# Pooled attention into a gated MLP on one core: Strassen units in the first product, upper groups first in the second, batch 2 as pooled rows

## Chip, core and metric

The kernel runs on one core of a Trainium2 chip. The metric is device time in microseconds (us): 296.05 us, the median of three runs (296.0 to 296.78). TensorE is called PE below, VectorE DVE, ScalarE ACT, GpSimd POOL and SyncE SP. PE and its weight loads (PEld) are separate rows of the profile.

## What is computed

```python
B, H, S, D = 8, 8, 576, 64            # attention; pool = 8, so 72 pooled keys
k_p = k.reshape(B, H, 72, 8, D).mean(axis=3)
v_p = v.reshape(B, H, 72, 8, D).mean(axis=3)
attn = softmax(q @ k_p.T / sqrt(D))   # 576 x 72 for each head
x = (attn @ v_p) -> (4608, 512)       # heads side by side
h = x @ w_in                          # 512 -> 2048
out = (h * sigmoid(h)) @ w_out        # 2048 -> 512, float32
```

Matrix operands are bf16 on the chip, sums are float32.

## The kernel before

**Tiles.** The 4608 tokens are worked through in nine tiles of 512 (NTT), t = 0 to 8. Each tile has two stages. `up` computes the hidden layer of the tile, h_T, in 16 groups of 128 hidden units: four matmuls of 128x512 a group (the four parts of d_model), then one Silu on ACT, which reads PSUM and writes h_T in bf16. `down` (tile 0) or `down_quarters` (tiles 1 to 8) computes the output rows.

**Second product.** `down_quarters` is Strassen's scheme (its form with fewer additions is kept in three PSUM tiles P, Q and R). The hidden layer is cut in four quarters (two halves of the tokens, two halves of the hidden units: groups 0 to 7 and 8 to 15), w_out likewise. Seven products replace eight. Each is 16 matmuls of 128x256; product n takes its left operand from h_sum[n] (a sum of two quarters of h_T, made on DVE by `hidden_sum(n, k0, k1)` for the groups k0 to k1 of a half) or from h_T, and its right operand from w_out or from w_sum (made once, by `weight_sum`). The order is 2, 5, 1, 4, 3, 7, 6. P, Q and R are used again as soon as DVE has read them: r_sb is a copy of product 2, rr_sb = Q + r_sb, t_sb = R - rr_sb, and o_sb gets P, Q, P + t_sb and Q + t_sb.

**Attention.** While PE works on tile t, it also does the attention of batch a = t + 1 (576 tokens each, so batches and tiles drift apart). Per batch: K and V are pooled on DVE, K is brought to kz (transposed by PE through kT_ps, copied by DVE), q is transposed by DVE in four parts (`q_transpose`), and four visits (two halves of the tokens f, two groups of four heads g) each do `scores` (PE, then four exponentials on ACT into es), `denominators` (PE into den_ps, then Ln and Exp on ACT into rec) and `numerators` (PE into nu_ps, then DVE into xT, which is the first product's input).

**Pooling.** Batches 0 and 1 are loaded as pooled rows (`load_slots`): row (head, pooled key) on the 128 partitions, five slots of them, its eight source rows side by side, 2 KB. `slot_sums` adds the eight on DVE in three steps, and small matmuls with an identity or a shift matrix (`select_k`, `select_v`) bring each head's 72 rows to where they are used. Batch 2 is loaded by `load_heads`, with 72 partitions and four heads in a tile (k_raw, k_raw2, v_raw, v_raw2), all eight source rows side by side, once w_out is there; `tree` (lines 197 and 208) adds them on DVE. Later batches are loaded by `load_one` (first four source rows) and `load_rest`, a DMA issued by POOL that adds the other four in flight, so that DVE has one step less.

**Order.** The order within an engine is written by hand. `up` and the downs count their matmuls in steps (64 and 112), and a list of fillers (f_up, f_down) says behind which step other work is put: (36, f) runs f behind step 36; what is left at the end runs then. Each engine works in the order in which the program emits its instructions, so a filler that waits holds up what is behind it on its engine. In `up` before, the groups go 0 to 15, the h_sums are put at steps 20 to 59, and four of them at the end.

**Buffers.** PSUM has eight one-bank tiles: three of tag mm (hp_ps, and P, Q, R of down) and five of tag at (attention). r_sb, rr_sb and t_sb exist once.

Of the kernel before, what the change touches and what calls it, by code (L numbers as in the profile page):

```python
# [27 lines left out]
FP32 = mybir.dt.float32  # L28
# [8 lines left out]
def kernel(  # L37
# [74 lines left out]


# [68 lines left out]

    def load_heads(b, name, tags, behind=None):
        st = batches.setdefault(b, {})
        st[f"{name}_raws"] = []
        for i, tag in enumerate(tags):
            raw = raw_tile(tag, H // 2)
            if behind is not None:
                nc.gpsimd.tensor_copy(out=raw[:, 0, :1], in_=behind)
            load_rows(nc.sync, raw, source(b, name)[:, i * H // 2 : (i + 1) * H // 2, :])  # L190
            st[f"{name}_raws"].append(raw)


    def tree(dsts, raw):
        w = raw.shape[2] // 2
        while w > D:
            nc.vector.tensor_add(  # L197
                out=raw[:, :, :w], in0=raw[:, :, :w], in1=raw[:, :, w : 2 * w]
            )
            w //= 2  # L200
        n = H // 2 if len(dsts) > 1 else raw.shape[1]
        for i, dst in enumerate(dsts):
            in0, in1 = (
                raw[:, i * n : (i + 1) * n, c * D : (c + 1) * D].rearrange(
                    "k h (c d) -> k h c d", c=2
                ) for c in range(2)
            )
            nc.vector.tensor_add(out=dst, in0=in0, in1=in1)


    def pooled(b, name, i):
        p = batches[b][f"{name}p"]
        if name == "k":
            return p[:, i].rearrange("k c s d -> k s c d")
        return p[:, i * H // 2 : (i + 1) * H // 2, :].rearrange(
            "k h (c d) -> k h c d", c=2
        )

    def pool_heads(b, name, i):
        tree([pooled(b, name, i)], batches[b][f"{name}_raws"][i])  # L220

    def pool_k(b, parts=(0, 1)):
        st = batches[b]
        st["kp"] = mid.tile([SP, 2, 2, 4, DH], BF16, tag="kp", bufs=1, name="kp")
        if "k_raws" not in st:
            tree([pooled(b, "k", i) for i in range(2)], st["k_raw"])
        else:
            for i in parts:
                pool_heads(b, "k", i)

    def pool_v(b, parts=(0, 1)):
        st = batches[b]
        st["vp"] = mid.tile([SP, H, D], BF16, tag="vp", name="vp")
        if "v_raws" not in st:
            tree(
                [st["vp"].rearrange("k h (c d) -> k h c d", c=2)], st["v_raw"]
            )
        else:
            for i in parts:
                pool_heads(b, "v", i)  # L240

    def k_transpose(b, parts=(0, 1)):
        st = batches[b]
        kT_ps = ps_tile([128, 2, 2, SP], BF16, "at", "kT_ps")
        for a in parts:
            for c in range(2):
                nc.tensor.transpose(
                    kT_ps[:, a, c, :],
                    st["kp"][:, a, c].rearrange("k s d -> k (s d)"),
                    ident[:SP, :SP],  # L250
                )
        a0, a1 = parts[0], parts[-1] + 1
        nc.vector.tensor_copy(out=kz[b % 2][:, a0:a1], in_=kT_ps[:, a0:a1])
# [14 lines left out]
            raw_tile(f"{n}_raw{i}", H, full=True)[:, : m * RE].rearrange(  # L268
                "r (i e) -> r i e", e=RE
            ) for i, m in (("", SA), (2, SLOTS + 1 - SA))  # L270
# [3 lines left out]
    def load_slots(eng, b, name, i0, i1):  # L274
        src = (k if name == "k" else v)[b].rearrange("h (sp p) d -> (h sp) (p d)", p=POOL)
        tiles = row_tiles[name]
        if i0 == SLOTS:
            eng.dma_start(out=tiles[1][:REST, SLOTS - SA], in_=src[128 * SLOTS :])
        else:
            j = i0 // SA  # L280
            eng.dma_start(
                out=tiles[j][:, i0 - SA * j : i1 - SA * j],
                in_=src[128 * i0 : 128 * i1].rearrange("(i r) e -> r i e", r=128),
            )

    def slot_sums(name, j):
        raw = row_tiles[name][j]
        dst = rows5[name][:, SA:] if j else rows5[name][:, :SA]
        w = RE // 2
        while w > D:  # L290
            nc.vector.tensor_add(  # L291
                out=raw[..., :w], in0=raw[..., :w], in1=raw[..., w : 2 * w]
            )
            w //= 2
        nc.vector.tensor_add(out=dst, in0=raw[..., :D], in1=raw[..., D : 2 * D])
# [120 lines left out]

    def up(t, fillers, items):
        step = spread(fillers, len(items) * KF)
        for g, n0, n in items:
            hp_ps = ps_tile([128, 512], FP32, "mm", "hp_ps")  # L420
            c0 = (t * NTT + n0) % NX

            for r0, r1 in ((0, min(n, NX - c0)), (min(n, NX - c0), n)):
                for kk in range(KF) if r1 > r0 else ():
                    if r0 == 0:
                        next(step)
                    x0 = (c0 + r0) % NX
                    nc.tensor.matmul(  # L428
                        hp_ps[:, r0:r1],
                        lhsT=w_in_sb[:, kk, g * 128 : (g + 1) * 128],  # L430
                        rhs=xT[:, kk, x0 : x0 + r1 - r0],
                        start=(kk == 0), stop=(kk == KF - 1),
                    )
            nc.scalar.activation(h_T[:, g, n0 : n0 + n], hp_ps[:, :n], func=AF.Silu)  # L434
        for _ in step:
            pass

# [84 lines left out]
    def down_quarters(t, fillers, last=False):  # L522
# [7 lines left out]
        def product(n, k0, k1, cs=(0, 1)):  # L530
            b = bank[n]
            for kt in range(k0, k1):
                for c in cs:
# [4 lines left out]
                        stop=kt == KQ - 1, skip_group_check=True,  # L538
# [5 lines left out]
        KA = KQ - 2  # L544
        product(2, 0, KA)
        product(5, 0, KA)
        product(2, KA, KQ)
        nc.vector.tensor_copy(out=r_sb, in_=ps["P"])
        product(5, KA, KQ)
        tt(out=rr_sb, in0=ps["Q"], in1=r_sb, op=add)  # L550
        for cc in ((0,), (1,)) if last else ((0, 1),):
# [4 lines left out]
            nc.vector.tensor_copy(out=o_sb[1][:, cs, LO], in_=ps["P"][:, cs])  # L556
# [105 lines left out]

    visits = [(f, g) for f in range(2) for g in range(2)]
    for t in range(NT):
# [11 lines left out]
        else:  # L676
            items = [(g, 0, NTT) for g in range(KG)]
            for n, k0, k1, at in (
                (6, 0, 4, 20), (6, 4, 8, 36),
                (2, 0, 4, 51), (5, 0, 4, 52), (1, 0, 4, 53), (2, 4, 6, 58), (5, 4, 6, 59),  # L680
            ):
                f_up.append((at, lambda n=n, k0=k0, k1=k1: hidden_sum(n, k0, k1)))
            f_up.append((64, lambda: hidden_sum(2, 6, 8)))
            f_up.append((64, lambda: hidden_sum(5, 6, 8)))
            f_up.append((64, lambda: hidden_sum(1, 4, 8)))
            f_down.append((27 if t < NT - 1 else 41, lambda: hidden_sum(7, 0, 8)))

        for n, t0, f_to, at in (
            (1, 0, f_down, 48), (3, 0, f_down, 54), (4, 1, f_up, 12),
            (7, 1, f_down, 10), (6, 1, f_down, 50),  # L690
        ):
            for i in range(PW):
                if t == t0:
                    f_to.append((at + i, lambda n=n, i=i: weight_sum(n, i)))
        if a < B:
            q_at = [20, 28, 36, 44] if t else [82, 84, 86, 88]
            if t == 0:
                for j in range(2):
# [5 lines left out]
                    f_down.append((37 + 3 * j, lambda j=j: copy_v(1, j)))  # L704
            else:
                f_up.append((0, lambda: pool_k(a)))
                f_up.append((25, lambda: k_transpose(a)))
            for n in range(4):
                f_up.append((q_at[n], lambda n=n: q_transpose(a, n // 2, n % 2)))
            if t == 1:  # L710
                f_up.append((46, lambda: pool_v(a, (0,))))
                f_down.append((30, lambda: pool_heads(a, "v", 1)))
            elif t:
                f_up.append((10, lambda: pool_v(a)))
            if t == 0:
                f_down.append((0, lambda: load_q(2)))

                last = w_out_sb[:SP, KG - 1, d_model - 1 :]
                f_down.append(
                    (1, lambda: load_heads(2, "k", ("k_raw", "k_raw2"), last))  # L720
                )
                f_down.append(
                    (14, lambda: load_heads(2, "v", ("v_raw", "v_raw2"), last))
                )
            elif a + 1 < B:
                f_v = f_up if t > 1 else f_down
# [3 lines left out]
                f_v.append((11 if t > 1 else 31, lambda: load_one(a + 1, "v")))  # L730
                f_v.append((12 if t > 1 else 32, lambda: load_rest(a + 1, "v")))
# [11 lines left out]
            for n, (f, g) in enumerate(visits):  # L743
                if n < 3 or not 3 <= t < B - 2:
                    f_down.append((nu_at[n], lambda f=f, g=g: numerators(a, g, f)))
# [36 lines left out]
```

The softmax here doesn't subtract the row's maximum and nothing guards it: scores larger than these inputs give would overflow.

## Time and profile before

| | us |
|---|---|
| device time, median of 3 | 296.05 |
| profiled span | 294.7 |
| PE busy | 287.9 |
| DVE busy | 191.2 |
| ACT busy | 177.6 |
| POOL busy | 42.8 |

The busy row of a page says how long an engine had something in work. Matmuls are pipelined, and their ends are modelled: a busy PE may still wait. Where it is full can be read from the distance between the starts of consecutive matmuls. The chain of waits follows the work back from the last instruction; a long run of one engine in it, with no other between, means that this engine alone set the time there. The table of stretches gives the busy time of each engine in each tile.

### The profile page before, as it was taken

The numbers are of one execution on the slowest core, as the hardware profiler recorded it, in microseconds if no ns is written. First come the engines' busy times: TensorE is split into PE (matmuls) and PEld (weight loads), VectorE is DVE, ScalarE is ACT, GpSimd is POOL, SyncE is SP. The second block draws the span as 40 slices with busy tenths as digits, with TensorE's granted clock in tenths as the row PEclk, the third lists the DMA queues.
The fourth block names the chain that finished last, engine by engine and source line by source line (L and its number), as shares of the span: only waits on it lengthen the run. The fifth ranks groups of instructions, "written<-read, shape, count | busy, mean of one in ns | idle before, by whom it ended". The sixth has DMA issues, their size and how long they took to land.

```text
span 294.7 us, 6052 instructions
## 1 busy us (share of the span) xinstructions
PE 287.9 (98%) x2417; PEld 175.6 (60%) x2417; DVE 191.2 (65%) x344; ACT 177.6 (60%) x366; POOL 42.8 (15%) x60
## 2 busy tenths in 40 slices
PE   8999999999999999999999999999999999999995
PEld 3348434446564666457788774476547654884584
DVE  4886445999978566865586659666865642741562
ACT  1677675567566865676667675776577666407500
POOL 8654100001300120013001710110000000000000
PEclk9999999999999999999999999999999999999998
DMA  7999999958794797487857895783500032004003
GB/s 215 271 282 205 247 229 180 209 147 174 106 177 108 160 132 136 106 177 111 150 128 162 120 122 137 167 116 51 123 20 2 2 89 53 2 22 117 6 12 135
DMA packets 34909, 37.65 MB, mean 128 GB/s; under 512 B 9856, under 2 KB 26368, under 8 KB 34880
## 3 DMA queue, kind: packets, MB, share of 16 engines
q0 software_dynamic: 20128, 18.50, 37.3%
q1 hardware_dynamic: 14176, 17.84, 26.5%
q10 hardware_dynamic: 576, 0.92, 0.9%
q8 instruction: 19, 0.31, 0.5%
q14 instruction: 10, 0.08, 0.1%
HBM read 36.70 MB, written 9.44 MB: 157 GB/s over the span
## 4 chain that ended last, share of the span: by engine, by line
PE 86%; DVE 10%; ACT 1%; issue 1%; DVEq 0%
PE hp_ps L428 37%; PE o_psQ L535 14%; PE o_psP L535 14%; PE o_psR L535 4%; PE sc_ps L348 4%; PE o_ps L462 4%; PE warm_ps L583 4%; PE nu_ps L388 3%; DVE raw L197 3%; DVE h_sum L495 2%; PE den_ps L365 2%; DVE w_sum L513 2%; DVE qT L148 1%; DVE xT L396 1%; PE kz_ps L313 1%
## 5 line engine op out<-in xcount | busy, mean ns | idle before, releaser
L428 PE MATMUL hp_ps<-xT,w_in_sb 128*128 128x512 bf16 (+3 forms) x684 | 128.2, 345 | 0.4 <-ACT h_T L434 0.4
L434 ACT ACTIVATE h_T<-hp_ps 128x512 bf16<-128x512 f32 (+2 forms) x155 | 87.4, 567 | 57.4 <-PE hp_ps L428 45.3
L428 PEld LDWEIGHTS <-w_in_sb 128*128 128x128 bf16 x684 | 65.9, 98 | 56.6 <-issue 1.5
L495 DVE TENSOR_TENSOR h_sum<-h_T 128x1024 bf16<-128x1024 bf16 (+2 forms) x88 | 52.0, 637 | 36.1 <-ACT h_T L434 36.1
L535 PEld LDWEIGHTS <-h_sum 128*128 128x128 bf16 x640 | 60.9, 98 | 15.1 <-issue 6.5
L356 ACT ACTIVATE es<-sc_ps 72x288 bf16<-72x288 f32 x128 | 41.4, 403 | 13.2 <-PE sc_ps L348 13.1
L396 DVE TENSOR_TENSOR xT<-nu_ps,rec 128x288 bf16<-128x288 f32 x64 | 25.7, 448 | 12.0 <-PE nu_ps L388 11.8
L535 PEld LDWEIGHTS <-h_T 128*128 128x128 bf16 x256 | 23.6, 98 | 6.5 <-issue 4.1
L177 POOL DMA_DIRECT2D raw<-in_k_dram x5 | 7.1, 1420 | 114.5 <-DVE h_sum L495 48.4
L148 DVE STREAM_TRANSPOSE qT<-q_bf 128x576 bf16<-128x576 bf16 x32 | 23.6, 758 | 0.0
L374 ACT ACTIVATE lnd<-den_ps 128x288 f32<-128x288 f32 x30 | 12.3, 411 | 16.6 <-PE nu_ps L388 9.8
L197 DVE TENSOR_TENSOR raw<-raw 72x1024 f32<-72x1024 f32 (+1 forms) x18 | 19.7, 1094 | 0.1
L291 DVE TENSOR_TENSOR raw<-raw 128x768 f32<-128x768 f32 (+3 forms) x16 | 10.5, 654 | 11.1 <-DMA raw<-in_v_dram 7.8
L535 PE MATMUL o_psP<-w_out_sb,h_sum 128*128 128x256 bf16 x128 | 17.6, 273 | 0.0
L535 PE MATMUL o_psQ<-w_out_sb,h_sum 128*128 128x256 bf16 x128 | 17.6, 273 | 0.0
L535 PE MATMUL o_psQ<-w_sum,h_T 128*128 128x256 bf16 x128 | 17.5, 274 | 0.0
L535 PE MATMUL o_psP<-w_sum,h_sum 128*128 128x256 bf16 x128 | 17.0, 273 | 0.5 <-DVE o_sb L556 0.5
L535 PE MATMUL o_psP<-w_sum,h_T 128*128 128x256 bf16 x128 | 16.5, 273 | 0.0
L535 PE MATMUL o_psR<-w_sum,h_sum 128*128 128x256 bf16 x128 | 16.5, 273 | 0.0
L462 PE MATMUL o_ps<-w_out_sb,h_T 128*128 128x512 bf16 x64 | 15.9, 381 | 0.0
L535 PE MATMUL o_psQ<-w_sum,h_sum 128*128 128x256 bf16 x128 | 15.4, 273 | 0.0
L348 PE MATMUL sc_ps<-qT,kz 32*72 32x288 bf16 x256 | 14.4, 295 | 0.9 <-DVE xT L396 0.7
(58 smaller groups left out, 212.0 us busy)
## 6 DMA issues: line engine op xcount, KB each, us to landing
out_dram<-o_sb SPq DMA_DIRECT2D x128, 64.0 KB, 1.7
raw<-in_k_dram SPq DMA_DIRECT2D x8, 512.0 KB, 5.2
raw<-in_v_dram SPq DMA_DIRECT2D x7, 512.0 KB, 6.9
q_bf<-in_q_dram POOLq DMA_DIRECT2D x6, 576.0 KB, 11.8
raw<-in_k_dram POOLq DMA_DIRECT2D x5, 576.0 KB, 9.1
raw<-in_v_dram POOLq DMA_DIRECT2D x5, 576.0 KB, 9.9
w_in_sb<-in_moe_w_in_dram POOLq DMA_DIRECT2D x8, 256.0 KB, 8.5
w_out_sb<-in_moe_w_out_dram POOLq DMA_DIRECT2D x4, 512.0 KB, 13.7
```

Source lines behind the costliest of these rows:

```text
L148: nc.vector.transpose(out=st["qT"][:, a, f * QF : (f + 1) * QF].rearrange("r i c p -> r (i c p)"), in_=st["q_bf"][:, a, f * n : (f + 1) * n],)
L197: nc.vector.tensor_add(out=raw[:, :, :w], in0=raw[:, :, :w], in1=raw[:, :, w : 2 * w])
L348: nc.tensor.matmul(sc[s], lhsT=kz[b % 2][rows, g, c, :], rhs=st["qT"][rows, g, f * QF : (f + 1) * QF, c, :], start=(c == 0), stop=(c == 1),)
L356: nc.scalar.activation(es[:, s, :], sc[s], func=AF.Exp, scale=score_scale)
L374: nc.scalar.activation(lnd, den_ps[:, :HS], func=AF.Ln)
L396: nc.vector.tensor_mul(out=xT[:, 2 * g + c, cols], in0=nu[c][:, :HS], in1=rec)
L428: nc.tensor.matmul(hp_ps[:, r0:r1], lhsT=w_in_sb[:, kk, g * 128 : (g + 1) * 128], rhs=xT[:, kk, x0 : x0 + r1 - r0], start=(kk == 0), stop= ...
L434: nc.scalar.activation(h_T[:, g, n0 : n0 + n], hp_ps[:, :n], func=AF.Silu)
L462: nc.tensor.matmul(ps, lhsT=h_T[:, g, m * 128 : (m + 1) * 128], rhs=w_out_sb[:, g, :], start=(g == 0), stop=(g == KG - 1),)
L495: nc.vector.tensor_tensor(out=h_sum[n][:, ks, :], in0=quarter(*a, ks), in1=quarter(*b, ks), op=op)
L535: nc.tensor.matmul(ps[b][:, c, :], lhsT=left(n, kt, c), rhs=W_OUT[n][:, kt, :], start=b not in begun, stop=kt == KQ - 1, skip_group_check= ...
L583: nc.tensor.matmul(warm_ps, lhsT=warm[:, :128], rhs=warm, start=True, stop=True)
```

## The change

The change does four things.

1. **Units in the first product.** From tile 2 on, groups 4 to 7 and 8 to 11 of `up` are each one Strassen unit. A unit is a product of two by two blocks: 256 hidden units twice, 256 of d_model twice, 256 tokens twice. Seven products of four 128x256 matmuls each replace 16 matmuls of 128x512. The weight sums (w_sum1, five for a unit) are made once, in tile 0's down; the sums of x (x_sum, five of them, used by both units) are made on DVE at the start of each tile's up. The additions behind the products use r_sb (now a copy by ACT), rr_sb, t_sb, and two new tiles c_sb, from which Silu reads two of the four blocks. P, Q and R of a unit are PSUM tiles of tag at. Stages of the units are put between plain groups: 12, 13, unit 0 "251", 14, "43", 15, "76", unit 1 "2", the last Silu of unit 0 ("s"), "51", group 0, "43", 1, "76", 2, "s", 3. Tile 1 has the plain groups in the order 12 to 15, 4 to 11, 0 to 3.
2. **Second product from its upper groups.** Products 2 and 5 begin with the upper half of their groups (4 to 7 and 12 to 15 of h_T), since groups 0 to 3 are now last in up. The h_sums are put accordingly.
3. **Batch 2 as pooled rows.** It is loaded as batches 0 and 1 are, but in two halves of each row, the second by an accumulating DMA (`load_half_2`), all on POOL's queue. `slot_sums` has one step less, and `select_k`, `select_v` take the place of the transpose.
4. **Copies from DVE to ACT, and places of fillers.** r_sb, one o_sb copy (but in the last tile) and the copy of kT_ps go to ACT. For batches 3 to 7, pooling of K is put at the end of the down before, pooling of V at the start of down. Three of four q transposes are at steps 15 to 17 of up, the fourth in down.

```diff
+    w_sum1 = [singles.tile([128, 5, 2, 256], BF16, name=f"w_sum1{n}") for n in range(2)]
+    x_sum = singles.tile([128, 5, 2, NQ], BF16, name="x_sum")
+    c_sb = [singles.tile([128, 2, NQ], FP32, name=f"c_sb{n}") for n in range(2)]
...
-        nc.vector.tensor_copy(out=kz[b % 2][:, a0:a1], in_=kT_ps[:, a0:a1])
+        nc.scalar.copy(kz[b % 2][:, a0:a1], kT_ps[:, a0:a1])
...
+        def product(y, n, bank, first):
+            if first:
+                ps[bank] = ps_tile([128, 2, NQ], FP32, "at", f"u_ps{bank}")
+            w, x = unit_weights(y, n), unit_x(t, n)
+            for u in range(2):
+                next(step)
+                for kk in range(2):
+                    nc.tensor.matmul(
+                        ps[bank][:, u, :], lhsT=w[:, kk, 128 * u : 128 * (u + 1)],
+                        rhs=x[:, kk, :], start=first and u == 0 and kk == 0,
+                        stop=kk == 1, skip_group_check=True,
...
+            if n == "2":
+                product(y, 2, "P", True)
+                nc.scalar.copy(r_sb, ps["P"])
+            elif n == "5":
+                product(y, 5, "Q", True)
+                tt(out=rr_sb, in0=ps["Q"], in1=r_sb, op=ALU.add)
+            elif n == "1":
+                product(y, 1, "R", True)
+                tt(out=t_sb, in0=ps["R"], in1=rr_sb, op=ALU.subtract)
+            elif n == "4":
+                product(y, 4, "P", False)
+                hidden(y, 1, 0, ps["P"])
+            elif n == "3":
+                product(y, 3, "Q", False)
+                hidden(y, 0, 1, ps["Q"])
+            elif n == "7":
+                product(y, 7, "P", False)
+                tt(out=c_sb[0], in0=ps["P"], in1=t_sb, op=ALU.add)
+                hidden(y, 0, 0, c_sb[0])
+            elif n == "6":
+                product(y, 6, "Q", False)
+                tt(out=c_sb[1], in0=ps["Q"], in1=t_sb, op=ALU.add)
+            else:
+                hidden(y, 1, 1, c_sb[1])
...
-        KA = KQ - 2
+        KA = KQ // 2
+        product(2, KA, KQ)
+        product(5, KA, KQ)
         product(2, 0, KA)
+        nc.scalar.copy(r_sb, ps["P"])
         product(5, 0, KA)
-        product(2, KA, KQ)
-        nc.vector.tensor_copy(out=r_sb, in_=ps["P"])
-        product(5, KA, KQ)
         tt(out=rr_sb, in0=ps["Q"], in1=r_sb, op=add)
...
+    def load_half_2(name, half):
+        for i0, i1 in ((0, SA), (SA, SLOTS), (SLOTS, SLOTS + 1)):
+            load_slots(nc.gpsimd, 2, name, i0, i1, half)
...
+            for n in (2, 5):
+                f_up.append((36, lambda n=n: hidden_sum(n, 4, 8)))
+            f_up.append((56, lambda: hidden_sum(6, 4, 8)))
+            for n, k0 in ((2, 0), (5, 0), (1, 4), (1, 0)):
+                f_up.append((64, lambda n=n, k0=k0: hidden_sum(n, k0, k0 + 4)))
+            f_down.append((33, lambda: hidden_sum(7, 0, 8)))
+            f_down.append((71, lambda: hidden_sum(6, 0, 4)))
...
+            q_at = [15, 16, 17, 49] if t else [82, 84, 86, 88]
...
+                f_down.append((0, lambda: load_half_2("k", 0)))
                 f_down.append((0, lambda: load_q(2)))
...
+                f_down.append((0, lambda: load_half_2("k", 1)))
+                for half in range(2):
+                    f_down.append((31, lambda half=half: load_half_2("v", half)))
+                for y in range(2):
+                    for n in U_W:
+                        f_down.append((6, lambda y=y, n=n: unit_weight_sum(y, n)))
             elif a + 1 < B:
-                f_v = f_up if t > 1 else f_down
+                f_down.append((80, lambda: pool_k(a + 1, 0)))
+                f_down.append((100, lambda: pool_k(a + 1, 1)))
```

## The prediction

> **What bounds the kernel now.** First the page's busy shares, then the chain of waits.
>
> ```profile
> PE 287.9 (98%) x2417; PEld 175.6 (60%) x2417; DVE 191.2 (65%) x344; ACT 177.6 (60%) x366; POOL 42.8 (15%) x60
> ...
> PE 86%; DVE 10%; ACT 1%; issue 1%; DVEq 0%
> ```
>
> PE is busy all the way and carries 86% of the chain. Busy alone doesn't say that it is full, so I read the chain in order of time at tile 7, which has no attention work:
>
> ```profile
> 238.30 13.81 PE hp_ps L428 x64
> 252.11 1.31 PE o_psP L535 x12
> 253.42 1.31 PE o_psQ L535 x12
> ...
> 255.60 1.75 PE o_psR L535 x16
> ```
>
> 13.81/64 = 0.2158 us from one 512-wide matmul to the next, 1.75/16 = 0.1092 us for a 256-wide one, no wait between. So a tile costs 64 x 0.2158 + 112 x 0.1092 = 26.04 us, and the table by stage (one row a tile, from tile 1 on) says the same:
>
> ```profile
> 51.80:86.02 34.22, 33.55 (x279) 19.32 (x278) 31.82 (x63) 22.27 (x44) 3.63 (x3) 1.00 0.85 161
> 86.02:116.58 30.56, 30.56 (x262) 18.23 (x260) 20.92 (x36) 20.62 (x42) 3.54 (x3) 1.00 0.73 138
> 116.58:146.67 30.09, 30.09 (x254) 18.23 (x253) 20.16 (x34) 20.62 (x42) 3.57 (x3) 1.00 0.73 135
> ...
> 238.30:264.34 26.04, 26.04 (x177) 17.23 (x176) 11.19 (x18) 10.84 (x17) 0.00 (x0) 1.00 0.18 43
> ```
>
> Columns after the stretch: length, then busy time of PE, weight loads, DVE, ACT, POOL. In tiles 2 to 7 PE busy equals the length. Time can come off only by taking work from PE. DVE has 9 to 10 us to spare in an attention tile, 15 in tile 7; in tile 1 it has 2.4. The 10% of DVE in the chain is tile 1, where a queue of DVE work ended in PE's one wait there:
>
> ```profile
> 77.39 0.40 PE L348 MATMUL sc_ps<-qT,kz 32*72 32x288 bf16 x5 [0.67 <-DVE xT L396]
> ```
>
> [...]
>
> **The units on PE.** A unit takes 16 matmuls of 512 (3.45 us) away and adds 7 products x 4 matmuls of 256, 28 x 0.1092 = 3.06: 0.395 less. Two units in each of tiles 2 to 8: 0.79 a tile, 5.53 in all if nothing waits.
>
> **The units on DVE and ACT.** From the groups by shape in tile 3, DVE alone:
>
> ```profile
> L495 DVE TENSOR_TENSOR h_sum<-h_T 128x512 bf16<-128x512 bf16 x4 | 1.5, 420 | 0.9 <-ACT h_T L434 0.9
> ...
> L548 DVE COPY r_sb<-o_psP 128x512 f32<-128x512 f32 x1 | 0.7, 692 | 1.5 <-PE o_psP L535 1.5
> ...
> L554 DVE TENSOR_TENSOR t_sb<-o_psR,rr_sb 128x512 f32<-128x512 f32 x1 | 0.7, 679 | 0.0
> L253 DVE COPY kz<-kT_ps 128x288 bf16<-128x288 bf16 x1 | 0.3, 308 | 0.0
> ```
>
> The numbers after the bar are busy us, mean ns, and the idle time before. DVE gains, per tile, five x_sum (128x512 bf16; same-shaped sums in L495 last 0.42, and four in a row took 1.42 in the w_sum group, so 0.34 to 0.36 each), 1.8, and four adds a unit from PSUM (0.69 each, 0.61 when one starts on the other's heels), 5.2. It loses r_sb, one o_sb copy and the kz copy to ACT (0.69 + 0.69 + 0.31) and about 0.3 of h_sum. Net +5 us on 20 to 21: 25 to 26 of 29.5, still below PE, but waits now matter. ACT gains four copies of 0.59 and kz: 20.6 to 23.3. A Silu that reads c_sb in SBUF isn't in the trace: at least the 0.60 of one from PSUM[...]; I take 0.60, since ACT isn't full.
>
> **Walk through one attention tile** (0 = first matmul of up; PSUM reaches its reader 0.2 after the last issue, as in tile 2: last issue of up at 99.8, last Silu at 100.01). The o_sb add of the tile ahead holds DVE to 0.8, then the x_sums end at 2.6, just as product 1 comes up (2.60; it needs only the first, ready at 1.25). r_sb is copied by 3.05, rr ready 3.8, t 4.5; products 4 (3.90) and 3 (4.34) don't wait. Then three q transposes (0.7 each) are in DVE's queue to 6.6, so c_sb[0], possible at 6.4, starts at 6.6 and is done at 7.3. Unit 1's product 5 needs that PSUM buffer (five in the pool) at 7.09: **0.25 us of wait**. r_sb of unit 1 stands behind the Silu of c_sb[0] on ACT: 8.5; rr 9.2, t 9.9; products 4 (9.1) and 3 (9.5) pass with 0.3 to 0.6 to spare. Up ends at 13.4 against 13.95 before (kT's 0.14 in both): **0.52 saved of 0.79**. For tiles 2 to 6: 2.6 us. Tiles 7 and 8 have no q transposes and no kT: c_sb[0] starts as product 7 leaves PSUM, and unit 1's buffers are free: 2 x 0.79 = 1.6.
>
> Down, counted from its start: DVE does the lower sums until 3.6, then pool_v (1.2 + 0.7), rr at 5.5 to 6.2, h_sum 7 to 7.4, two xT, t to 8.9, q, xT, the lower half of h_sum 6 to 11.2, the o_sb copy of Q at 11.7, pool_k's first add to 13.6, xT, the add of P, kp to 15.8, and the last add at 16.3 against 16.1, where product 6 has left PSUM. The products that wait behind these: 3 on rr (asked for at 8.9), 7 on h_sum 7 (11.5), 6 on the o_sb copy (13.8). So DVE is level with PE again at the tile's end, by 0.2 us; that is the thinnest place of the walk.
>
> **Second product.** Its upper groups are first because groups 0 to 3 are now last in up. The last Silu starts 0.4 after up's end instead of 0.2 (the Silu of c_sb[1] is ahead of it), the lower sums of products 2 and 5 are ready at about 1.7 and 2.4 after it, and PE asks for them at 2.1 and 3.0. The first den_ps needs the es of four heads: table load 1.28 and es 1.30 behind that Silu put it at 3.6, PE comes at 3.7 (before, in tile 2's timeline: es done 103.22, den_ps at 103.54). Nothing on PE: hidden by 16 matmuls of upper groups and eight of scores, but with 0.1 to 0.6 us to spare. r_sb on ACT stands behind the es and before lnd; rec still has a microsecond before nu_ps. In the last tile r_sb on ACT shortens the chain r_sb, rr, t, copy into the 0.52 wait of o_psP: -0.15.
>
> **Batch 2 as rows (tile 1).** DVE loses the trees of L197/L208 (9.2 us) and gains slot sums and copies of 128 rows, 3.3 + 1.5. PE gains 24 + 12 selecting matmuls and loses kT: in tile 0 the same took 0.21 + 0.57 and 0.20 + 0.41, so 1.4 less 0.14, +1.25. The 0.67 wait should go, -0.67. The numerators of the first visit now want vp, which is behind h_sum 7 on DVE: step 48 comes 49 x 0.109 + 0.74 (two scores) + 0.45 (two den_ps) + 0.6 (v's selection) = 7.1 us into down, vp after 3.6 (h_sums) + 1.6 (slot sums) + 0.7 (rr) + 1.2 (h_sum 7) + 0.4 = 7.5: +0.35. The transfer: v of batch 1 landed at 40.1, w_out at 43.6; then k's first half, q (1.2 MB) and, once the first half has landed, k's second half with the add. The page's table of DMA issues has such an accumulating load:
>
> ```profile
> raw<-in_k_dram POOLq DMA_DIRECT2D x5, 576.0 KB, 9.1
> ```
>
> 9.1 us from issue to landing, so 46 to 47 + 9 is about 56. The slot sums are at the head of tile 1 on DVE (54.2), behind them the w_sums and q transposes; PE asks for k5 at 58.8 and for the first h_sums at 68.3. Two us late is absorbed, what is beyond is paid. Value taken: 1.25 - 0.67 + 0.35 = **+0.9** (bounds: +0.4, vp in time and selection at 1.1; and +4, the half 5 us late). The ten w_sum1 adds (3.4 us) fall into DVE's 7.20 wait for batch 1's v (32.9 to 40.1): nothing.
>
> **Sum.** -2.6 - 1.6 - 0.15 + 0.9 = -3.4: 296.05 - 3.4 = **292.6 us**.
>
> **Rivals.**
> (1) Nothing waits: my 0.25 is an artefact of placing q too strictly, and all seven tiles save 0.79. For: DVE's real pitch in a row is 0.07 below its durations. -5.5 - 0.15 + 0.4: 290.8.
> (2) DVE becomes the bound in tiles 2 to 6. For: about 25.5 us of DVE in 29.5, in strict order, with rr, t and c_sb each having a matmul behind it; DVE waited 1.4 to 3 us for h_T at the end of each up before. Against: it has 4 us. The five tiles gain nothing: -1.6 - 0.15 + 0.9: 295.2.
> (3) DVE falls behind and the lag is carried over: x_sums start a microsecond late, unit 0's rr holds product 3, the last Silu comes late and den_ps waits for es; 0.5 lost in each of five tiles, and k's second half is 3 us late: +2.5 - 1.75 + 3 gives 299.8. For: the margins of 0.1 to 0.6 above; POOL waits for landings in order. Against: slack before in every one of these places.
>
> **Chances.** The forecast 0.47, (1) 0.24, (2) 0.16, (3) 0.13. Predicted is the forecast's 292.6. The range goes from 290.5 (a little under rival 1) to 296.4 (rival 2 with its tile 1 a microsecond worse); left out are rival 3 and a sliver below. Faster by over 0.3% (below 295.2): forecast, rival 1 and half of rival 2: 0.80. Within 0.3%: 0.07. Slower: 0.13.
>
> **What would show it.** Tiles 7 and 8: up of 13.0 us with no gap. Tiles 2 to 6: DVE 25 to 26 us, PE waiting 0.2 to 0.3 at the products of unit 1, on DVE c_sb. Tile 1: DVE waits for raw until about 56, no PE wait at kz_ps. Wrong if den_ps waits on ACT, if u_psQ waits on rr_sb, if kz_ps waits for DVE and DMA, or if DVE idle in tiles 2 to 6 is near zero.

## The result, and the profile after

| | before | after |
|---|---|---|
| device time, median (range), us | 296.34 (296.0 to 296.78) | 294.05 (293.2 to 294.46) |
| ratio, with its 95% interval | 1 | 0.9918 (0.9889 to 0.9947) |

The change saves 2.3 us where 3.4 were forecast. (Medians and ranges of the runs below leave out three executions that were in a slow state, at 298.2, 300.7 and 303.6 us.) First the page of the changed kernel: busy time of each engine, and the chain of waits by engine.

```profile
PE 282.9 (97%) x2565; PEld 188.7 (65%) x2585; DVE 222.3 (76%) x408; ACT 187.4 (64%) x400; POOL 52.2 (18%) x68
...
PE 25%; DVE 1%; issue 0%; ACT 0%
```

PE has 5 us less to do, DVE 31 us more. The 25% says nothing: the chain could be followed back only to 213 us of 291, and all of what it covers is PE. So the tiles have to be read one by one. The table by stage, one row a tile (tiles 1 to 4, 6 and 7; after the stretch its length, then busy PE, weight loads, DVE, ACT, POOL):

```profile
53.63:87.02 33.39, 32.27 (x291) 19.02 (x292) 24.89 (x54) 23.20 (x46) 6.80 (x7) 1.00 0.72 128
87.02:116.98 29.96, 29.85 (x284) 20.53 (x284) 25.47 (x45) 21.95 (x47) 3.53 (x3) 1.00 0.57 113
116.98:146.28 29.30, 29.20 (x276) 20.50 (x276) 23.23 (x39) 22.05 (x47) 3.52 (x3) 1.00 0.76 144
146.28:176.60 30.32, 30.01 (x318) 23.80 (x317) 25.97 (x47) 21.97 (x47) 1.39 (x1) 1.00 0.68 127
...
206.28:237.23 30.95, 30.31 (x292) 20.71 (x293) 26.41 (x49) 21.96 (x47) 0.00 (x0) 1.00 0.22 47
237.23:262.51 25.28, 25.18 (x200) 19.38 (x200) 16.41 (x27) 12.22 (x21) 0.00 (x0) 1.00 0.18 42
```

The same rows of the kernel before, for tiles 4 and 6:

```profile
146.67:177.16 30.49, 30.49 (x325) 24.62 (x324) 20.79 (x36) 20.62 (x42) 8.14 (x10) 1.00 0.94 133
207.50:238.30 30.80, 30.80 (x269) 18.40 (x268) 21.65 (x38) 20.64 (x42) 0.00 (x0) 1.00 0.14 34
```

Every tile from 2 to 8 had two units put in. Tile 3 went from 30.09 us to 29.30, tile 7 from 26.04 to 25.28; but tile 4 only from 30.49 to 30.32, and tile 6 from 30.80 to 30.95. In those two, busy PE falls short of the length by 0.3 and 0.6 us (0.1 in tile 3): PE waits. In tile 1 it falls short by 1.1. The next table splits each tile into up and down, at the start of each stage's first matmul; its last column is after less before. (Some records of matmuls are missing from the trace. Where that of a stage's first one is missing, the boundary is set 0.22 us, one 512-wide matmul, ahead of the next record.)

| tile | up before | up after | down before | down after | change |
|---|---|---|---|---|---|
| 1 | 14.10 | 15.93 | 17.55 | 17.46 | +1.74 |
| 2 | 13.95 | 13.15 | 16.61 | 16.81 | -0.60 |
| 3 | 13.95 | 13.16 | 16.14 | 16.14 | -0.79 |
| 4 | 14.11 | 13.93 | 16.39 | 16.39 | -0.18 |
| 5 | 13.95 | 13.29 | 16.39 | 16.39 | -0.66 |
| 6 | 13.95 | 14.10 | 16.85 | 16.85 | +0.15 |
| 7 | 13.81 | 13.02 | 12.23 | 12.27 | -0.75 |
| 8 | 13.81 | 13.02 | 13.07 | 12.58 | -1.28 |

The sum is -2.37, close to the difference of the medians, -2.29. That closeness is in part chance: the two profiled spans, 294.7 and 291.4, differ by 3.3. Of the microsecond between, 0.6 lies ahead of tile 0's first matmul, at 17.75 and 17.19, and nearly all the rest behind the last one. In the profiles of the experiments below that first matmul starts anywhere from 17.1 to 18.1, so no part of the change is read from it.

**The units, where nothing waits.** The timeline of PE in tile 3 of the changed kernel (start, length, what ran; a wait would stand in brackets at the end):

```profile
118.71 0.60 PE L459 MATMUL u_psP<-xT,w_sum 128*128 128x256 bf16 x4
119.15 0.60 PE L459 MATMUL u_psQ<-xT,w_sum 128*128 128x256 bf16 x4
119.58 0.60 PE L459 MATMUL u_psR<-x_sum,w_sum 128*128 128x256 bf16 x4
120.02 1.03 PE L517 MATMUL hp_ps<-xT,w_in_sb 128*128 128x512 bf16 x4
```

Products start 0.435 us apart, four times 0.109, and up takes 13.02 plus the 0.14 of kT (K's transpose): the whole 0.79 is there. In tile 4 the plain groups run as matmuls of 256 columns in both kernels, so two units take away 64 of those and add 56: 8 x 0.109 = 0.87 is to be had there.

**Tiles 4 to 6.** DVE's timeline where tile 5 ends and tile 6 begins (206.28):

```profile
205.10 1.22 DVE L187 TENSOR_TENSOR raw<-raw 72x1024 f32<-72x1024 f32 x1 [2.02 <-DMA raw<-in_k_dram]
206.24 0.81 DVE L378 TENSOR_TENSOR xT<-nu_ps,rec 128x288 bf16<-128x288 f32 x2
206.97 0.68 DVE L653 TENSOR_TENSOR o_sb<-o_psP,t_sb 128x512 f32<-128x512 f32 x1
207.57 0.74 DVE L192 TENSOR_TENSOR kp<-raw 72x256 bf16<-72x256 f32 x2
208.24 0.68 DVE L657 TENSOR_TENSOR o_sb<-o_psQ,t_sb 128x512 f32<-128x512 f32 x1
208.84 1.75 DVE L427 TENSOR_TENSOR x_sum<-xT 128x512 bf16<-128x512 bf16 x5
210.51 0.68 DVE L479 TENSOR_TENSOR rr_sb<-u_psQ,r_sb 128x512 f32<-128x512 f32 x1
```

The delay begins in the first line: the first step of pooling K waits 2.02 us for the accumulating DMA that brings K's second half. Everything below it stands behind it in DVE's queue and is held up. The add of P (L653) sets free the PSUM tile that up needs for its third group, so PE waits there, 0.40 us:

```profile
207.70 1.02 PE L517 MATMUL hp_ps<-xT,w_in_sb 128*128 128x512 bf16 x4 [0.40 <-DVE o_sb L653]
```

and later once more for rr_sb of a unit. The list of waits has three such waits for K, at the ends of tiles 3, 4 and 5, and their cost is in the ups of tiles 4, 5 and 6:

```profile
DVE raw L187 <- DMA raw<-in_k_dram: 5.0, 3, 2.0
```

(us in total, times, longest.) Why K is late is in the queue of SP's DMAs in tile 3. First before, then after:

```profile
115.95 9.27 SPq L450 DMA_DIRECT2D out_dram<-o_sb  x16
125.34 1.17 SPq L168 DMA_DIRECT2D raw<-in_k_dram  x2
...
116.54 12.94 SPq L537 DMA_DIRECT2D out_dram<-o_sb  x16
129.58 1.92 SPq L172 DMA_DIRECT2D raw<-in_k_dram  x2
```

In both kernels the load of K's first half is emitted behind the 16 stores of the tile before. These now take until 129.5, so K's load begins 4.2 us later. POOL starts the adding half at 136.57 (131.62 before), and it is in at 144.9, when DVE goes on. Besides, pooling of K was moved forward, from the next tile's start to the end of this down. Before, this was its first step:

```profile
147.32 1.21 DVE L197 TENSOR_TENSOR raw<-raw 72x1024 f32<-72x1024 f32 x1
```

An estimate shows that it took both. Before, with the median of 9.1 us from issue to landing, K was in at about 140.7 and had 6.6 us to spare. After, it is in 4.2 us later (144.9), and DVE comes to the step 4.2 us earlier (143.1): 6.6 - 8.4 gives the wait of 1.8 us that this tile's end shows.

**Tile 1.** PE's timeline, and DVE's beside it:

```profile
58.63 0.28 PE L295 MATMUL kz_ps<-shifts,k 128*32 128x72 bf16 x12
59.06 0.81 PE L517 MATMUL hp_ps<-xT,w_in_sb 128*128 128x512 bf16 x3 [0.16 <-issue]
60.78 0.64 PE L295 MATMUL kz_ps<-shifts,k 128*32 128x72 bf16 x12 [0.91 <-DVE kz L302]
```

```profile
54.24 0.55 DVE L273 TENSOR_TENSOR raw<-raw 128x384 f32<-128x384 f32 x1
...
58.81 0.38 DVE L600 TENSOR_TENSOR w_sum<-w_out_sb 128x512 bf16<-128x512 bf16 x1
59.11 1.42 DVE L152 STREAM_TRANSPOSE qT<-q_bf 128x576 bf16<-128x576 bf16 x2
60.47 0.27 DVE L302 CAST kz<-kz_ps 128x144 bf16<-128x144 f32 x1
```

The second selection of K writes the PSUM tile that the copy of the first one reads. That copy stands behind w_sums and three q transposes, and starts at 60.47, 1.6 us after the selection. K itself is no trouble: the slot sums begin at 54.24 without a wait for a DMA.

**In short:** tile 7's up went from 13.81 to 13.02; in tiles 4 to 6 a late DMA, through DVE's queue, takes most of the gain back; and tile 1 pays 1.74.

### The profile page after: what moved, and what is told of

Its sections match the earlier page's. It is cut to its first block, busy times and chain, and to the rows that moved or that the text cites. A ratio compares the mean times of both kernels' runs of the same rounds, so it can differ in the third digit from the quotient of the medians.

```text
span 291.4 us, 6563 instructions
## 1 busy us (share of the span) xinstructions
PE 282.9 (97%) x2565; PEld 188.7 (65%) x2585; DVE 222.3 (76%) x408; ACT 187.4 (64%) x400; POOL 52.2 (18%) x68
## 5 line engine op out<-in xcount | busy, mean ns | idle before, releaser
L517 PE MATMUL hp_ps<-xT,w_in_sb 128*128 128x512 bf16 (+3 forms) x413 | 83.6, 340 | 1.9 <-DVE o_sb L653 0.6
L523 ACT ACTIVATE h_T<-hp_ps 128x512 bf16<-128x512 f32 (+2 forms) x99 | 53.7, 548 | 36.7 <-PE hp_ps L517 35.7
L582 DVE TENSOR_TENSOR h_sum<-h_T 128x1024 bf16<-128x1024 bf16 (+1 forms) x72 | 50.9, 743 | 12.3 <-ACT h_T L523 12.3
L517 PEld LDWEIGHTS <-w_in_sb 128*128 128x128 bf16 x428 | 40.7, 98 | 28.1 <-issue 2.5
L459 PEld LDWEIGHTS <-w_sum 128*128 128x128 bf16 x280 | 27.3, 98 | 7.1
L467 ACT ACTIVATE h_T<-c_sb 128x512 bf16<-128x512 f32 x28 | 17.6, 628 | 10.4 <-DVE c_sb L491 10.4
L152 DVE STREAM_TRANSPOSE qT<-q_bf 128x576 bf16<-128x576 bf16 x32 | 23.0, 753 | 0.1
L273 DVE TENSOR_TENSOR raw<-raw 128x384 f32<-128x384 f32 (+3 forms) x20 | 12.4, 619 | 8.1 <-DMA raw<-in_v_dram 4.4
L187 DVE TENSOR_TENSOR raw<-raw 72x1024 f32<-72x1024 f32 x10 | 12.2, 1215 | 5.0 <-DMA raw<-in_k_dram 5.0
L529 POOL DMA_DIRECT2D out_dram<-o_sb x1 | 0.6, 626 | 83.5 <-issue 83.5
```

Source lines behind the costliest of these rows:

```text
L152: nc.vector.transpose(out=st["qT"][:, a, f * QF : (f + 1) * QF].rearrange("r i c p -> r (i c p)"), in_=st["q_bf"][:, a, f * n : (f + 1) * n],)
L187: nc.vector.tensor_add(out=raw[:, :, : 2 * D], in0=raw[:, :, : 2 * D], in1=raw[:, :, 2 * D :])
L273: nc.vector.tensor_add(out=raw[..., :w], in0=raw[..., :w], in1=raw[..., w : 2 * w])
L459: nc.tensor.matmul(ps[bank][:, u, :], lhsT=w[:, kk, 128 * u : 128 * (u + 1)], rhs=x[:, kk, :], start=first and u == 0 and kk == 0, stop=kk ...
L467: nc.scalar.activation(h_T[:, g : g + 2, j * NQ : (j + 1) * NQ], src, func=AF.Silu)
L517: nc.tensor.matmul(hp_ps[:, r0:r1], lhsT=w_in_sb[:, kk, g * 128 : (g + 1) * 128], rhs=xT[:, kk, x0 : x0 + r1 - r0], start=(kk == 0), stop= ...
```

## The experiments

**Theory A:** the units pay in full wherever nothing waits, and two waits, both from the order within a queue, take the rest: K's second half (A1: because of the place of K's load in SP's queue behind the stores), and the copy of kz in tile 1. **Theory B:** DVE is nearly full (25 us of 29.5, in strict order), so that any delay on it reaches PE, and what shows as a wait for K would show elsewhere if K were early. The kernel before was run beside each group: 296.25 in the first, 296.33 in the second, 296.37 in the third.

**The changed kernel again.**

> The changed kernel again, as the measure for the others of its group: 293.5 to 294.5 us, up of tiles 2 and 3 at 13.2 us, of tiles 4 and 6 at 13.9 to 14.1. If the longer ups are scatter of one execution, they move to other tiles.

Measured: 294.81 us (293.67 to 295.83), ratio 0.9950 (0.9932 to 0.9968). Against the 296.25 beside it this is a gain of 1.4 us, not 2.3. Its list of waits:

```profile
DVE raw L187 <- DMA raw<-in_k_dram: 4.9, 2, 3.3
...
PE hp_ps L517 <- DVE o_sb L653: 1.6, 1, 1.6
```

Here K is late twice instead of three times, one of them by 3.3 us; the up of tile 4 takes 15.38, that of tile 5 13.15, that of tile 6 13.74. Tiles 2 and 3 are at 13.15 again. So the loss moves about between tiles 4 and 6 from run to run, and the kernel's time with it: against ups of 13.23, 13.15 and 13.15, which the next run reaches, this profile loses 2.7 us there, the first one 1.8.

**Pooling of K later.**

```diff
-                f_down.append((80, lambda: pool_k(a + 1, 0)))
+                f_down.append((95, lambda: pool_k(a + 1, 0)))
```

> pool_k's first add moved from step 80 to step 95 of down, behind the o_sb add of P. Theory A (tiles 4 to 6 lose their gain because this add waits on DVE for the accumulating load of K, with the o_sb add and the x_sums queued behind it): the DVE waits for raw shrink to under 0.3, up of tiles 4 to 6 goes to 13.2 to 13.3, and the time falls by 1.4 to 1.9 us against the changed kernel. Theory B (DVE is simply near full, 76% busy, and the order of two of its instructions doesn't matter): same sum of DVE work, less than 0.4 us of difference.

Measured: 292.53 (292.15 to 293.03), 0.9885 (0.9868 to 0.9901), 2.3 us under the run above. No wait for K on DVE is left; ups of tiles 4 to 6 13.23, 13.15, 13.15, with the same work on DVE. That is what A says and B forbids. Yet tiles 2 and 3 grew to 13.50. Unit 1 in tile 3, PE:

```profile
126.21 0.60 PE L459 MATMUL u_psP<-x_sum,w_in_sb 128*128 128x256 bf16 x4
126.93 0.60 PE L459 MATMUL u_psQ<-x_sum,w_in_sb 128*128 128x256 bf16 x4
```

0.72 between products instead of 0.435: product 3 waits 0.29 for rr_sb, because the moved 1.2 us add now stands ahead of the x_sums and all that follows them. 0.3 of the 1.2 us comes through to PE: at this place DVE has about 0.9 us of slack. In tiles 4 to 6, where the same add was moved, product 3 doesn't wait: DVE comes to the x_sums 1.59 us after the start of up there, and only after 1.96 in tiles 2 and 3.

**q transposes behind the copies of kz, in tile 1 only.**

```diff
-            q_at = [15, 16, 17, 49] if t else [82, 84, 86, 88]
+            q_at = [82, 84, 86, 88] if t == 0 else [27, 28, 29, 49] if t == 1 else [15, 16, 17, 49]
```

> Tile 1's three q transposes moved from steps 15 to 17 to steps 27 to 29 of up, behind both kz copies. Theory A (PE's second selection of K waits for the first kz copy, which stands behind w_sums and q transposes on DVE): the 0.9 us wait of kz_ps goes, up of tile 1 from 15.9 to about 15.0, time -0.8 to -0.9 us. Theory B (DVE work of tile 1 is the bound, 12 w_sums and 3 transposes having moved into its up): the wait comes back at the first product of down or at sc_ps, under 0.3 us gained.

Measured: 293.08 (292.04 to 293.77), 0.9890 (0.9871 to 0.9910). Tile 1's up is 14.96, 0.97 less, and the wait is gone from PE's timeline:

```profile
59.25 0.28 PE L295 MATMUL kz_ps<-shifts,k 128*32 128x72 bf16 x12
59.46 1.04 PE L517 MATMUL hp_ps<-xT,w_in_sb 128*128 128x512 bf16 x4
60.42 0.64 PE L295 MATMUL kz_ps<-shifts,k 128*32 128x72 bf16 x12
```

Tile 1's down stays at 17.46, so the wait doesn't come back there. Tiles 4 to 6 still wait for K (13.66, 14.04, 13.62). The median lies 1.7 us under the changed kernel's; 0.97 of it is tile 1, the rest is K's wait, which varies.

**No units.** Plain groups in all tiles from 1 on, no x_sums; all else as changed.

```diff
-            if t == 1:
+            if t >= 1:
                 items = G(
...
-            if t > 1:
+            if t > NT:
                 for n in U_X:
```

> Tiles 2 to 8 with 16 plain groups in the order of tile 1, no x_sums (the weight sums stay); everything else as changed. Theory A (the units' matmuls are paid in full, 0.79 a tile, where DVE is on time): up of tiles 2, 3, 7, 8 back to 13.95 and 13.81; tiles 4 to 6 also at 14.0, since without the x_sums and unit adds the late o_sb add meets slack; 294.05 + 4 x 0.79 + (0.2 + 0.7 - 0.1) gives 297 to 298 us. Theory B (units pay little because DVE fills up): under 295.5.

Measured: 299.02 (297.9 to 300.49), 1.0101 (1.0076 to 1.0125): slower than before the change, and slower than I expected. Tiles 2, 3, 7 and 8 have ups of 13.95, 13.95, 13.81 and 13.81, as before; tiles 4 to 6 have 14.24, 14.35 and 15.32, for K is late here too:

```profile
DVE raw L187 <- DMA raw<-in_k_dram: 5.1, 3, 2.4
```

With DVE at 174.9 us busy, 47 less than with units, these three ups lose 1.9 us together (14.11, 13.95 and 13.95 before), as much as with units in the first run. So the wait for K needs neither the units nor a full DVE. The units themselves are worth 299.02 - 294.81 = 4.2 us in this company, with K's wait in both kernels.

**K's first half ahead in SP's queue.** The load of the next but one batch's K is emitted at step 101 of the down before, between that tile's stores.

```diff
-                f_up.append((1, lambda: load_one(a + 1, "k")))
+                if t == 1:
+                    f_up.append((1, lambda: load_one(a + 1, "k")))
+                if a + 2 < B:
+                    f_down.append((101, lambda: load_one(a + 2, "k")))
```

> pool_k's add stays at step 80; instead the plain first half of K for batches 4 to 7 is issued at step 101 of the down before (it was step 1 of up), so on SP's queue it stands ahead of the last eight stores of that tile instead of behind them. Theory A1 (K lands late because its load stands behind 16 stores on SP, which take 9 to 14 us of that queue): K's first half is issued some 5 us earlier, DVE's wait for raw at step 80 goes to zero, tiles 4 to 6 save as tiles 2 and 3; 292.5 to 293.0 us. Theory A2 (the accumulating half on POOL is late for its own reasons, it waits for V and q ahead of it): DVE still waits over 1 us in tiles 4 to 6, time as changed, 294 to 295.

Measured: 292.19 (292.05 to 292.39), 0.9861 (0.9846 to 0.9877). SP's queue in tile 3:

```profile
116.67 5.27 SPq L537 DMA_DIRECT2D out_dram<-o_sb  x8
123.50 1.17 SPq L172 DMA_DIRECT2D raw<-in_k_dram  x2
124.91 5.97 SPq L537 DMA_DIRECT2D out_dram<-o_sb  x8
```

K's load starts 6.1 us earlier than in the changed kernel, POOL's adding half 6.7 us earlier (129.91 against 136.57). DVE no longer waits for the K of batches 3 to 7; the ups of tiles 2 to 6 are 13.15, 13.16, 13.23, 13.15 and 13.29, and the four runs lie within 0.4 us of each other, where the nine of the changed kernel spread over 2.2. Moving one load in one queue gives back 2.6 us (or 1.9 against the first run of the changed kernel), with pooling left at its step 80. A1 is shown: the order in SP's queue made K late, and with the load moved the early pooling costs nothing.

**A dose of DVE.** Two h_sums of tiles 2 to 6 are made twice: the same values, 0.69 us each.

```diff
             f_down.append((71, lambda: hidden_sum(6, 0, 4)))
+            if 2 <= t <= 6:
+                f_up.append((57, lambda: hidden_sum(6, 4, 8)))
+                f_down.append((72, lambda: hidden_sum(6, 0, 4)))
```

> Two h_sum instructions of tiles 2 to 6 are done twice (0.61 us each, upper half of 6 at step 57 of up, lower half at step 72 of down): ten more, 6.1 us of DVE work. Theory A (DVE has idle time at those places, waits are what costs): under 0.6 us more than the changed kernel. Theory B (DVE is the bound of the attention tiles): 3 to 6 us more.

Measured: 294.83 (294.47 to 295.56), 0.9954 (0.9938 to 0.9971), against 294.81 of the changed kernel. The groups by shape in tiles 2 and 3 show the dose taken:

```profile
L582 DVE TENSOR_TENSOR h_sum<-h_T 128x1024 bf16<-128x1024 bf16 x20 | 13.1, 686 | 0.7 <-ACT h_T L523 0.5
```

13.1 us where the changed kernel has 10.3, and the ups of both tiles stay at 13.15, the downs at 16.82 and 16.14. The clean test is tile 2, with the up of tile 3: in the downs of tiles 3 to 5 the second dose stands ahead of the place where K comes late and can hide in that wait. Theory B falls: DVE has at least 1.4 us to spare in a tile, at these two places (at the place of the moved add it had 0.9).

**r_sb of the last tile on DVE again.**

```diff
-        nc.scalar.copy(r_sb, ps["P"])
+        (nc.vector.tensor_copy if last else nc.scalar.copy)(r_sb, ps["P"])
```

> In the last tile r_sb is copied by DVE again. If the 0.49 us that down of tile 8 saved come from taking this copy out of DVE's chain r_sb, rr, t, o_sb copy, they are lost: down of tile 8 from 12.58 to 13.0 to 13.1, the wait of o_psP from 0.15 to 0.5 to 0.7. If they come from h_sum 7 or from the order of the products: no change.

Measured: 294.39 (293.32 to 295.34), 0.9934 (0.9924 to 0.9944). The scatter from K hides half a microsecond in the medians; the last down doesn't wait for K and shows it: 12.99 against 12.58, so 0.41 of the 0.49 is lost again, with the old wait back.

```profile
PE o_psP L622 <- DVE o_sb L644: 0.4, 1, 0.4
```

**Pooling later and q transposes later together.** The edits of both.

> The late first add of K (step 95) and the transposes behind the kz copies together. If the two waits are separate, both gains add: up of tile 1 at 15.0 and no wait in tiles 4 to 6, 292.5 - 0.95 = 291.6 us. If taking one away only brings out the other (DVE's queue being shifted as a whole), 292.3 or more.

Measured: 292.06 (291.08 to 292.31), 0.9850 (0.9831 to 0.9869). Tile 1's up is 14.96, tiles 4 to 6 don't wait, but tiles 2 and 3 have their 0.29 again (13.49): each edit does by itself what it did alone.

**K's load ahead and q transposes later together.**

> K's first half issued at step 101 of the down before, and the transposes of tile 1 behind the kz copies; pool_k's add stays at step 80. If the early load alone ends the waits of tiles 4 to 6 and the late add of the run with both edits costs tiles 2 and 3 a wait of 0.3 each (unit 1's product 3 for rr_sb), this one has up of 13.15 in both and 292.2 - 0.95 = 291.2 us. If 292.06 was the floor for another reason: 292.

Measured: **291.43** (291.41 to 291.72), 0.9833 (0.9820 to 0.9846), the lowest median of all, 2.6 us under the change and 4.9 under before. Its page:

```profile
PE 282.7 (98%) x2565; PEld 189.1 (65%) x2585; DVE 222.7 (77%) x408; ACT 187.6 (65%) x400; POOL 52.2 (18%) x68
...
PE 94%; ACT 3%; DVE 1%; issue 1%; DVEq 0%
```

The chain is PE to 94%, more than the 86% of before, with DVE as busy as in the changed kernel. Ups: 14.95, then 13.15, 13.15, 13.23, 13.16, 13.29, 13.03 and 13.02. Both waits are out. What is left: the last down is 12.91 in the profiles of both kernels with K's load ahead, against 12.58 of the change. In both, the last add into c_sb[0] starts 1.04 us after its product 7 does, in the change 0.69; the last h_sums come later with it, and product 2 waits 0.16 for them. What holds that add isn't settled.

**Batch 2 as the later batches are.** K's load ahead, and batch 2 loaded in 72 partitions with the second half added by DMA, pooled by `pool_k` and `pool_v`, K transposed by PE; no slot sums, no selections.

```diff
-                    f_up.append((0, lambda j=j: slot_sums("k", j, halves=True)))
-                    f_up.append((21 + 4 * j, lambda j=j: select_k(2, j)))
...
+                f_up.append((0, lambda: pool_k(2, 0)))
+                f_up.append((0, lambda: pool_k(2, 1)))
+                f_up.append((22, lambda: k_transpose(2)))
+                f_down.append((10, lambda: pool_v(2)))
...
-                f_down.append((0, lambda: load_half_2("k", 0)))
+                f_down.append((0, lambda: load_one(2, "k", nc.gpsimd)))
...
+                f_down.append((0, lambda: load_rest(2, "k")))
```

> Early K load as above; batch 2 loaded and pooled as batches 3 to 7 are (72 partitions, first half plain, second half added in DMA, both on POOL's queue; k_transpose), no slot sums and no selecting matmuls in tile 1. If the +1.7 of tile 1 came from the selections and their wait for kz: up of tile 1 at 13.95, down at 16.8, so 1.98 + 0.6 less than with the early load alone: 289.6 us. If K of batch 2 on 72 partitions comes later than 54 us, or DVE's adds hold up the h_sums, the loss comes back as a wait of kT_ps or at the start of down: 291 or more.

Measured: 293.06 (291.24 to 294.42), 0.9881 (0.9851 to 0.9910), so 0.9 over the same kernel with rows (292.19), in intervals that overlap, and far from 289.6. The profile shows why it isn't the gain that fewer PE and DVE instructions promise; DVE in tile 1:

```profile
60.72 1.22 DVE L187 TENSOR_TENSOR raw<-raw 72x1024 f32<-72x1024 f32 x1 [4.73 <-DMA raw<-in_k_dram]
```

and the transpose on PE behind it:

```profile
62.45 0.57 PE L221 MATMUL kT_ps<-shifts,kp 72*128 72x72 bf16 x4 [1.88 <-DVE kp L192]
```

K of batch 2 is in at 60.7 in this form, while its rows were there by 54.2. POOL's timeline shows where: it starts the adding half after a wait for the first, of 12.87 us and up to 49.3 here (loads started at 30.9 and 33.2), of 6.41 us and up to 44.6 with rows (30.1, 32.6 and 34.9). In this profile tile 0's down also waits 1.4 us for w_out, and whether that belongs to the edit isn't settled. K of batch 3, too, comes 1.7 us late at the end of tile 1, and tile 2's up takes 14.04. In this profile the rows cost instructions, and buy 6 us in the time of arrival. What the selections cost tile 1 beside the wait for kz is therefore still a count of matmuls, not the result of a run.

**The same without units.** The edits of the two kernels "no units" and "batch 2 as the later batches are".

> The same with plain groups in tiles 2 to 8 (no x_sums): prices the units with no other wait in tiles 2 to 8. Units paid in full: 7 x 0.79 = 5.5 us more than with them, 295.1 if that one is at 289.6. Units paid by two thirds, as the forecast had it for tiles 2 to 6: 4.2 more.

Measured: 297.2 (296.17 to 299.4), 1.0031 (1.0009 to 1.0052): 4.2 over the kernel with units, where 5.5 were expected. Its ups in tiles 3 to 8 are 13.95, 14.11, 13.95, 13.95, 13.82 and 13.81, against 13.15, 13.24, 13.16, 13.16, 13.02 and 13.02 with units. Now no tile from 3 on waits for K, and each shows 0.79 to 0.87 (the 0.87 is tile 4): 0.79 a tile is what the units are worth. The medians don't show the full sum. Both kernels scatter by 3 us, and K of batch 2 and of batch 3 is late in both by amounts that differ: tiles 1 and 2 have ups of 17.15 and 15.17 here, 16.43 and 14.04 with units.

## Why the prediction was right, and where it was not

| step | forecast | measured |
|---|---|---|
| units, tiles 7 and 8 | -1.58 | -1.54 |
| tiles 2 to 6 | -2.6 | -2.08 |
| tile 1 | +0.9 | +1.74 |
| last down | -0.15 | -0.49 |
| sum | -3.4 | -2.37 |

(Tile 8's -1.28 is split into -0.79 of its up and -0.49 of its down. The terms missed by +0.04, +0.52, +0.84 and -0.34.)

**Right: PE sets the time, and a unit saves 0.395.** Tiles 7 and 8 came to 13.02 with no gap. The end of 294.05 lies in the range, on the side forecast. The range is wide, though: it takes in rival 2, whose mechanism the runs refute.

**Tiles 2 to 6: the term was near by luck.** It was 0.52 a tile, from a wait of 0.25 at unit 1's product 5. That wait came nowhere: in tile 3 c_sb[0] starts 6.5 us after the start of up (6.6 in the walk), its record ends at 7.16, and product 5 starts at 7.08 without a gap, as rival 1 had it. Why the buffer was free before the end of that record isn't settled. Instead tiles 2 and 3 took the whole 0.79, and tiles 4 to 6 only 0.18, 0.66 and -0.15. The step that failed is "pool_k's first add to 13.6": the walk gave it DVE time and asked for no data. Its transfer was never followed, although the page of before held what was needed (9.1 us from issue to landing, and SP's and POOL's queues in the timeline). The diff moved K's use 4.2 us forward, the longer stores put its load 4.2 us back, and I had costed both at nothing. I looked for DVE's margin where it was thin, 0.2 us; the 2 us came from a wait in front of that.

**DVE as the bound (rival 2): no.** It has 23.2 to 26.4 us in an attention tile (25 to 26 forecast), and in tile 2 a dose of 1.4 us cost nothing. Part of rival 3 was right in kind: a late DVE held product 3 by rr_sb, and a second half of K came late. But it was the K of batches 5 to 7, not of batch 2. Of the four signs that the prediction named as speaking against it, three came in small: den_ps and u_psQ waited, and kz_ps did, for DVE alone and not for a DMA.

**Tile 1: the term was mis-sized by 0.84.** K of batch 2 was forecast for 56 and was in by 54.2, so there was no late half; and the forecast had PE not waiting at kz_ps, where it waited 0.91 for a copy held up in DVE's order. The walk counted DVE's load in this tile, not the place of this copy behind the transposes. Moving those took 0.97 off. By stage the miss is larger: the terms put 0.64 in up and 0.29 in down, and up got 1.83, down -0.09. The 0.67 wait of sc_ps is gone, as forecast.

**Small ones.** den_ps did wait for es, in tile 2 only: its four matmuls, from 103.91 to 104.35, take 0.2 more than in other places, and the last es ends at 104.09; the margin had been put at 0.1. Without the units, and in the kernel with batch 2 on 72 partitions, tile 2's down takes 16.60 as before; an order made to avoid the wait wasn't tried. The last down gained 0.49, not 0.15: r_sb on ACT takes a DVE instruction and its place in the queue out of the chain to the o_psP wait, 0.52 before and 0.15 now. The Silu that reads c_sb lasts 628 ns:

```profile
L467 ACT ACTIVATE h_T<-c_sb 128x512 bf16<-128x512 f32 x28 | 17.6, 628 | 10.4 <-DVE c_sb L491 10.4
```

This is 31 ns over the 597 of a Silu from PSUM in the kernel before, which the prediction took as the least and counted with. The trace of before had a sign of it: at 128x288 a Silu and lnd's Ln, both from PSUM, last 411 ns there, rec's Exp, from lnd in SBUF, 443; 32 more on the 597 gives an estimate of 629. ACT has room for it: it came to 22.0 us in tile 3, where 23.3 had been added up. Instructions in a row overlap there: after c_sb[0]'s Silu of 0.63 us, at 124.17, r_sb's copy starts 0.54 later.

Put together: units in full (-5.5), tile 1 (+1.7), den_ps (+0.2), the last down (-0.5), K (+1.8 here, up to 2.7) give -2.3 here. Without K's wait they give -4.1, and the kernel with K's load ahead measured 292.19 - 296.33 = -4.1 (-3.7 by the tiles of its one profile, whose last down gained 0.16).

## What to carry to other kernels

When a walk through an engine's queue puts an instruction at a time, write down next to it which data it needs and when these land: an instruction with no wait before may get one when its place is moved forward or when its load starts later (in tile 3 both, by 4.2 us each, and the first step of pooling K waited 1.81 us). Here a prefetch emitted behind 16 stores in one queue started when they had got through (129.58), and 6.1 us earlier when it was put between them (123.50): so look where a prefetch stands among the stores. And read a loss by tile: equal work with unequal times pointed to a wait here, and a wait that moved from tile to tile between runs (ups of 13.93, 13.29 and 14.10 in tiles 4 to 6, then 15.38, 13.15 and 13.74) came from a transfer.

## What had not been expected of the hardware

The stores of a tile went from 1.7 to 2.5 us from issue to landing on the page (median), and 16 of them took 12.94 us of SP's queue instead of 9.27, in tile 3:

```profile
out_dram<-o_sb SPq DMA_DIRECT2D x128, 64.0 KB, 2.5
```

Why isn't settled. It isn't the units: without them the stores take 12 us of the queue in that tile, and 2.6 to land. With K's load ahead they take 3.4 us to land, and the kernel is 2 us faster: here the time that the stores take was no cost by itself, only what waited behind them was.
